# A fp32 Strassen mixture of experts on one core: the order of ScalarE's, VectorE's and the loads' work in its first pass

## The chip, the cores and the metric

The kernel runs on one core of a Trainium2 chip. The metric is the device time of one execution in microseconds (us). Engines: TensorE (PE, its weight loads PEld), VectorE (DVE), ScalarE (ACT), GpSimd (POOL), and SyncE (SP), which issues most DMAs.

## What is computed

A banded attention (4 batches, 8 heads, 768 positions, head width 64) gives `x` of 3072 rows by 512. `x` goes through a mixture of 8 experts, all of them for every row, with Sinkhorn-balanced weights `P`:

```
logits = x @ w_gate
logits = logits - logits.max()
P = np.exp(logits)
for _ in range(8):
    P /= P.sum(1, keepdims=True) + 1e-09
    P /= P.sum(0, keepdims=True) + 1e-09
    P *= N / E
for e in range(E):
    h = np.maximum(x @ w1[e], 0.0)   # w1[e]: 512 x 1024
    ye = h @ w2[e]                   # w2[e]: 1024 x 512
    out += P[:, e:e + 1] * ye
```

Everything is fp32 at the door and in the result. The case is about the experts.

## The kernel before

**Products.** The hidden units are cut into groups of 256 (31 groups, numbered 0 to 30; the first 256 units are done with the attention), the rows into three passes of 1024. A group's first layer (`x @ w1`) and its second layer (`h @ w2`) are each done as a Strassen product: seven products instead of eight, `m1` to `m7` for the first layer and `p1` to `p7` for the second, whose operands are sums and differences of quarter blocks. Each operand is held as a high part in a reduced fp32 form (`fp32r`) and a low part, the fp32 value less the high part, so one product is two output banks of three matmuls 128x128 by 512 (low by high, high by low, high by high): six matmuls.

**Stages.** The attention and the groups 0 to 3 come first. Then the first pass, the subject here: rows 0 to 1023, groups 4 to 29, taken in 13 chunks of two groups. The weights come raw from DRAM in this pass and are turned into blocks on the fly; the finished blocks are also stored to DRAM (`w_spill`), and the two later passes only load them. Group 30 closes each pass.

**The order on TensorE.** The function `plan` (L1731) yields: seven products of an even group, then p6, p4, p2 of the chunk before for its two groups (13 products: here half B), then seven of the odd group and p3, p7, p5, p1 of this chunk for its two groups (15: half A). Each engine's queue is in order: where the code uses `Ordered` (a wrapper that keeps program order on an engine) the instructions stand in the order in which the code is run.

**First layer** (`layer1_held`, L880). Products go to four PSUM banks `a` to `d`, in the order m3, m2, m1, m6, m5, m4, m7. VectorE sums them, applies relu and the expert's share, and forms operands; `high` is a cast on ScalarE, `rest` the subtraction that gives the low part, on VectorE. p6, p4 and p2 have their casts in a tail, run step by step (`tails`) while p3 to p1 of the odd group run. For even groups, p2's low part goes to POOL through the list `chores`. After each product stands `done(m)`.

**Second layer** (`held_second`, L1676). It uses two PSUM banks a product, for two groups. p3, p7, p6 and p4 are seeded: ScalarE copies the running sums into the banks (`seed`), TensorE adds to them, and ScalarE copies them back (`evict`). p5, p1 and p2 are not seeded; VectorE adds their banks to the sums. An eviction is issued when the next product of that layer, or the next first layer, comes up.

**Weight blocks** (`maker`, L1494). A generator: for each group and layer two parts, four blocks and three. POOL forms sums of the raw tile, ScalarE casts the high parts, POOL subtracts for the low parts, and SP stores the tile. `tick` (L1548) adds the time of a product, `SLOT`, to `clock[0]` and lets the maker run until its own `clock[1]` is ahead; a part is begun when `clock[0]` has come within `LEAD` (L52) of the product that uses it. Raw tiles come by `fetch` (L1448) into three tiles, on SP's queue in order; the first three are fetched when the maker starts.

Names in the trace: most instructions are recorded at L70 (the wrapper), matmuls at L126. `bank_a` to `bank_d` are the first layer's banks, `c_acc` the second layer's, `early` the running sums and the sums t3 and t4, `raw` the raw tiles, `ext` extra sums of them, `w` a tile of weight blocks, `p` and some of `x` operands of the second layer, `x` and `m` those of the first, `full` h22, h11 and d5.

Of the kernel before, what the change touches and what calls it, by code (L numbers as in the profile page):

```python
# [50 lines left out]
SLOT = 1.36  # L51
LEAD = {(0, 0): (15, 15), (0, 1): (15, 15), (1, 0): (17, 18), (1, 1): (14, 16)}  # L52
BIAS = ((None, (32, 256), (128, 352)), ((0, 384), (32, 256), (128, 352)))
# [545 lines left out]
class Moe:  # L599
# [279 lines left out]

    def layer1_held(self, x, blocks, share, full, ops, tmp, ps, tag, done, even):  # L880

# [17 lines left out]

        product("m3", "c", True, False)  # L900
        copy(out=t3, in_=c)
        done("m3")
        product("m2", "d", True, False)
        tt(out=t3, in0=t3, in1=d, op=ALU.subtract)
        done("m2")
        product("m1", "a", True, False)
        tt(out=t4, in0=a, in1=t3, op=ALU.add)
        done("m1")
        product("m6", "b", True, True)
        tt(out=b, in0=b, in1=t4, op=ALU.add)  # L910
        scaled(h22, b, 1)
        done("m6")
        product("m5", "c", False, True)
        tt(out=t3, in0=t3, in1=c, op=ALU.subtract)
        scaled(c, c, 1)
# [3 lines left out]
        rest("p3", c)  # L919
        done("m5")  # L920
        product("m4", "d", False, True)
        tt(out=t3, in0=d, in1=t3, op=ALU.add)
        scaled(d, d, 0)
# [3 lines left out]
        rest("p7", b)  # L927
        done("m4")
        product("m7", "a", False, True)
        tt(out=a, in0=a, in1=t3, op=ALU.add)  # L930
        scaled(h11, a, 0)
        rest("p1", d)
        rest("p5", d5)
        tt(out=c, in0=c, in1=d5, op=ALU.subtract)
        tt(out=a, in0=c, in1=h11, op=ALU.subtract)
        done("m7")
        yield
# [6 lines left out]
        high("p2", h11)  # L944
        if even:
            done(lambda: rest("p2", h11, Ordered(self.tc, nc.gpsimd).tensor_tensor))
        else:
            rest("p2", h11)

# [116 lines left out]
def pipeline(tc, attention, ident, moe, acc, scratch):  # L1066
# [12 lines left out]
    with ExitStack() as top:  # L1079
# [368 lines left out]
        def fetch(n, g, layer, part):  # L1448

            e, f = groups[g]  # L1450
# [40 lines left out]

        clock, hurry, ready, chores = [0.0, 0.0], [False], set(), []

        def maker():  # L1494
# [29 lines left out]
            for b in wanted:  # L1524
# [3 lines left out]
                clock[1] = max(clock[1], clock[0])  # L1528
                while chores:
                    chores.pop(0)()  # L1530
                    clock[1] += 1.3
                t = ring_tile(part)
# [28 lines left out]
        def first_layer(p, g):  # L1561
# [16 lines left out]
            if p == 0 and g < NG - 1:  # L1578
                return moe.layer1_held(ops, lambda i: block(g, 0, i), share, (full[0], full[3], full[4]), ops_of[g], tmp, mps, "h", done, g % 2 == 0)

# [83 lines left out]
        def done(m):  # L1664
            if callable(m):
                chores.append(m)
                return
            if m == "m3":
                if tails:
                    next(tails.pop(), None)  # L1670
                evict()
            if m == "m1" and seeds_next:
                seed(seeds_next.pop())
            tick()

        def held_second(gs, ks, ends=False):  # L1676
            begins = gs is chunks_of[0][0]
            seeded = () if begins or ends else SEEDED
            for n, k in enumerate(ks):
                if n and tails:  # L1680
                    next(tails[0], None)
                evict()
                if n + 1 < len(ks) and ks[n + 1] in seeded:
                    seed(ks[n + 1])
                while k == "p2" and chores:
                    chores.pop(0)()
                if k not in banks_of:
# [12 lines left out]
        def held(n, what, p, x, y):  # L1700
            if what == "first":
                follows, _, gs, ks = todo[n + 1]
                if follows == "second" and gs is not chunks_of[0][0] and ks[0] in SEEDED:
                    seeds_next.append(ks[0])
# [66 lines left out]
        hurry[0] = False  # L1771
        clock[1] = 3.0
        load_share(0, groups[PLAIN][0])
# [109 lines left out]
```

## Time and profile before

| | |
|---|---|
| time, median of 3 runs | 2187.73 us (2186.73 to 2188.72) |
| profiled execution | 2188.77 us, span 2187.0 us |
| mean granted TensorE clock | 0.99 of full speed |
| PE busy | 2081.3 us (95%), 10365 matmuls |
| DVE busy | 1420.2 us (65%) |
| ACT busy | 844.3 us (39%) |
| POOL busy | 1577.3 us (72%) |
| DMA | 477.49 MB, mean 218 GB/s |

In the trace "x6" at a row's end counts the instructions it joins; in brackets stands the idle time of the engine before the row and what ended it. Times are us from the span's start. A matmul's duration is modelled from its start on and overlaps the next.

### The profile page before, as it was taken

The page shows a single profiled execution, that of the slowest core. Times are in us where ns is not written, and L with a number is a line of the kernel's source. Part 1 is how long each engine was busy: PE and PEld are TensorE (multiplying, and loading weights), DVE is VectorE, ACT ScalarE, POOL GpSimd, SP SyncE. Part 2 cuts the span into 40 slices and gives each one's busy share as a digit, 9 for nine tenths or more (in the row PEclk, how much of TensorE's full clock was granted, in tenths as well). Part 3 has the DMA queues.
Part 4 walks back from the last instruction along what each step waited for, and adds up shares of the span by engine and source line. Part 5 has one row for each costly group of instructions (what it writes and reads, how often), then busy time and mean ns, then how long its engine had stood idle before and what let it go on. Part 6 is the DMA issues. An engine that isn't in the chain of part 4 may idle for free.

```text
span 2187.0 us, 30410 instructions
## 1 busy us (share of the span) xinstructions
PE 2081.3 (95%) x10365; PEld 1712.6 (78%) x10365; DVE 1420.2 (65%) x2526; ACT 844.3 (39%) x1772; POOL 1577.3 (72%) x1405
## 2 busy tenths in 40 slices
PE   8999997888989899899999999999999999999999
PEld 6888885667767677677888888888888888888887
DVE  8777776576676767675565555665656666655566
ACT  7778531455555555523222222222142222222221
POOL 6787973677677776785767677776767776767776
PEclk9999998999999999999999999999999999999999
DMA  6777575567666676688565555656875656555564
GB/s 151 207 224 200 161 286 187 202 226 256 250 225 228 244 247 240 245 303 319 196 214 200 190 203 197 208 185 217 294 287 184 208 200 210 202 199 198 188 208 143
DMA packets 229157, 477.49 MB, mean 218 GB/s; under 512 B 107072, under 2 KB 152576, under 8 KB 205696
## 3 DMA queue, kind: packets, MB, share of 16 engines
q1 hardware_dynamic: 228704, 474.40, 63.5%
q8 instruction: 84, 1.38, 0.3%
q0 software_dynamic: 288, 1.05, 0.1%
q14 instruction: 81, 0.66, 0.1%
HBM read 328.75 MB, written 146.64 MB: 217 GB/s over the span
## 4 chain that ended last, share of the span: by engine, by line
PE 77%; DVE 8%; POOL 5%; ACT 4%; issue 4%; DMA 2%; SPq 0%; ACTq 0%; DVEq 0%; POOLq 0%
PE c_acc L126 33%; PE bank_a L126 9%; PE bank_d L126 9%; PE bank_c L126 9%; PE bank_b L126 5%; POOL w L70 3%; PE o_t L126 2%; PE o_ps L126 1%; DVE full L70 1%; DVE p L70 1%; ACT p_sb L371 1%; PE s_ps L126 1%; DVE early L70 1%; PE y_ps L126 1%; DMA ws<-w 1%
## 5 line engine op out<-in xcount | busy, mean ns | idle before, releaser
L126 PE MATMUL c_acc<-p,w 128*128 128x512 f32 x2838 | 691.4, 395 | 35.1 <-POOL w L70 25.7
L126 PEld LDWEIGHTS c_acc<-p,w 128*128 128x128 f32 x2838 | 538.2, 190 | 160.6 <-POOL w L70 29.9
L1640 DVE TENSOR_TENSOR early<-early,c_acc 128x512 f32<-128x512 f32 x308 | 210.8, 688 | 180.4 <-PE c_acc L126 180.4
L126 PE MATMUL bank_c<-x,w 128*128 128x512 f32 x1068 | 274.5, 392 | 14.0 <-ACT w L70 8.2
L70 POOL TENSOR_TENSOR early<-raw,full 128x512 f32<-128x512 f32 x56 | 72.8, 1300 | 288.0 <-DVE raw L793 288.0
L126 PE MATMUL bank_d<-x,w 128*128 128x512 f32 x1068 | 272.9, 391 | 0.7 <-DMA x<-op_m 0.7
L126 PE MATMUL bank_a<-m,w 128*128 128x512 f32 x1068 | 271.8, 390 | 1.3 <-DMA m<-op_m 0.7
L796 ACT CAST p<-raw 128x512 fp32r<-128x512 f32 x150 | 93.1, 620 | 417.3 <-DVE raw L793 328.4
L70 POOL TENSOR_TENSOR w<-raw,w 128x512 fp32r<-128x512 f32 (+2 forms) x107 | 187.5, 1752 | 82.9 <-ACT w L70 82.9
L126 PEld LDWEIGHTS bank_c<-x,w 128*128 128x128 f32 x1068 | 201.7, 189 | 57.7 <-ACT w L70 8.6
L126 PEld LDWEIGHTS bank_d<-x,w 128*128 128x128 f32 x1068 | 201.6, 189 | 43.3 <-DMA x<-op_m 1.2
L126 PEld LDWEIGHTS bank_a<-m,w 128*128 128x128 f32 x1068 | 200.6, 188 | 44.0 <-DVE x L70 1.1
L126 PE MATMUL c_acc<-x,w 128*128 128x512 f32 x774 | 199.5, 393 | 31.5 <-ACT c_acc L70 15.9
L70 POOL TENSOR_TENSOR p<-raw,p 128x512 fp32r<-128x512 f32 x152 | 196.5, 1293 | 3.5 <-ACT p L796 3.4
L126 PEld LDWEIGHTS c_acc<-x,w 128*128 128x128 f32 x774 | 143.5, 188 | 70.1 <-ACT early L70 20.6
L70 POOL TENSOR_TENSOR p<-full,p 128x512 fp32r<-128x512 f32 x120 | 155.9, 1299 | 3.7 <-ACT p L796 3.7
L70 POOL TENSOR_TENSOR x<-full,x 128x512 fp32r<-128x512 f32 x72 | 93.0, 1292 | 66.5 <-ACT x L70 66.5
L804 DVE TENSOR_TENSOR early<-early,bank_d 128x512 f32<-128x512 f32 x63 | 43.3, 688 | 150.1 <-PE bank_d L126 150.1
L796 ACT CAST p<-full 128x512 fp32r<-128x512 f32 x121 | 75.1, 621 | 160.9 <-POOL full L70 140.4
L126 PE MATMUL bank_b<-m,w 128*128 128x512 f32 x534 | 135.5, 389 | 0.0
L126 PEld LDWEIGHTS bank_b<-m,w 128*128 128x128 f32 x534 | 100.2, 188 | 20.9
L371 ACT ACTIVATE p_sb<-p_sb,mx 128x256 f32<-128x256 f32 (+1 forms) x188 | 90.5, 484 | 22.7 <-DVE mx L366 22.1
(384 smaller groups left out, 3792.4 us busy)
## 6 DMA issues: line engine op xcount, KB each, us to landing
w<-ws SPq DMA_DIRECT2D x124, 1024.0 KB, 4.9
w<-ws SPq DMA_DIRECT2D x122, 768.0 KB, 4.3
ws<-w SPq DMA_DIRECT2D x54, 1024.0 KB, 4.6
ws<-w SPq DMA_DIRECT2D x53, 768.0 KB, 5.7
raw<-in_moe_w_dram SPq DMA_DIRECT2D x54, 512.0 KB, 4.4
x<-p_rows SPq DMA_DIRECT2D x21, 512.0 KB, 4.9
x<-op_m SPq DMA_DIRECT2D x16, 512.0 KB, 10.3
ws<-w SPq DMA_DIRECT2D x4, 1792.0 KB, 8.5
```

What stands on the lines that cost most here:

```text
L70: return lambda *args, **kw: self.tc.keep_in_program_order(op(*args, **kw))
L126: return self.tc.keep_in_program_order(self.engine.matmul(*args, **kw))
L371: scalar.activation(out=views[u], in_=views[u], func=AF.Exp, bias=mx[:, u:u + 1], scale=-1.0, accum_out=sm[:, i, j:j + 1])
L796: engine.copy(out=ops[k][:, 0], in_=src)
L804: tt(out=t3, in0=t3, in1=d, op=ALU.subtract)
L1640: nc.vector.tensor_tensor(out=sums[k][q], in0=sums[k][q], in1=bank, op=ALU.add)
```

## The change

Five edits, all for the first pass.

1. `done(m)` stands right behind its product, ahead of the copies and sums that read its bank. In `done`, an eviction stands ahead of the tail's next step; in `held_second` too.
2. Seeds: both seeded products of the coming chunk part are now seeded in the first layer, at m1 and at m6 (before: the first at m1, the others one product ahead in `held_second`).
3. p2's low part is done on VectorE for even groups too; the list `chores` goes. p5's low part stands ahead of p1's, and both ahead of the sums with m7.
4. The first three raw loads are issued by `nc.sync` itself, not by the ordered queue, so that their place on SP is the scheduler's.
5. `LEAD` is raised in seven of eight entries, and `clock[1]` starts at 2.0 instead of 3.0.

```
@@ -49,7 +49,7 @@
 SEEDED = ("p3", "p7", "p6", "p4")
 SLOT = 1.36
-LEAD = {(0, 0): (15, 15), (0, 1): (15, 15), (1, 0): (17, 18), (1, 1): (14, 16)}
+LEAD = {(0, 0): (17, 17), (0, 1): (16, 15), (1, 0): (20, 21), (1, 1): (16, 18)}
...
@@ -898,42 +898,42 @@
             engine(out=ops[k][:, 1], in0=src, in1=ops[k][:, 0], op=ALU.subtract)
 
         product("m3", "c", True, False)
+        done("m3")
         copy(out=t3, in_=c)
-        done("m3")
         product("m2", "d", True, False)
+        done("m2")
         tt(out=t3, in0=t3, in1=d, op=ALU.subtract)
-        done("m2")
         product("m1", "a", True, False)
+        done("m1")
         tt(out=t4, in0=a, in1=t3, op=ALU.add)
-        done("m1")
         product("m6", "b", True, True)
+        done("m6")
         tt(out=b, in0=b, in1=t4, op=ALU.add)
         scaled(h22, b, 1)
-        done("m6")
         product("m5", "c", False, True)
+        done("m5")
         tt(out=t3, in0=t3, in1=c, op=ALU.subtract)
         scaled(c, c, 1)
         high("p3", c)
         tt(out=b, in0=c, in1=h22, op=ALU.subtract)
         high("p7", b)
         rest("p3", c)
-        done("m5")
         product("m4", "d", False, True)
+        done("m4")
         tt(out=t3, in0=d, in1=t3, op=ALU.add)
         scaled(d, d, 0)
         tt(out=d5, in0=h22, in1=d, op=ALU.subtract)
         high("p5", d5)
         high("p1", d)
         rest("p7", b)
-        done("m4")
         product("m7", "a", False, True)
+        done("m7")
+        rest("p5", d5)
+        rest("p1", d)
         tt(out=a, in0=a, in1=t3, op=ALU.add)
         scaled(h11, a, 0)
-        rest("p1", d)
-        rest("p5", d5)
         tt(out=c, in0=c, in1=d5, op=ALU.subtract)
         tt(out=a, in0=c, in1=h11, op=ALU.subtract)
-        done("m7")
         yield
         high("p6", c)
         rest("p6", c)
@@ -942,10 +942,7 @@
         rest("p4", a)
         yield
         high("p2", h11)
-        if even:
-            done(lambda: rest("p2", h11, Ordered(self.tc, nc.gpsimd).tensor_tensor))
-        else:
-            rest("p2", h11)
+        rest("p2", h11)
 
     def layer1_strassen(self, x, w, hs, tmp, ps, tag, sums_first, beat):
 
@@ -1447,6 +1444,7 @@
 
         def fetch(n, g, layer, part):
 
+            queue = nc.sync if n < 3 else Ordered(tc, nc.sync)
             e, f = groups[g]
             raw = raw_tiles[n % 3]
...
@@ -1526,9 +1524,6 @@
                 while clock[0] < used_at[b] - LEAD[layer, part][g % 2] and not hurry[0]:
                     yield False
                 clock[1] = max(clock[1], clock[0])
-                while chores:
-                    chores.pop(0)()
-                    clock[1] += 1.3
                 t = ring_tile(part)
                 sums, parts = recipe(raw_tiles[raw_of[b] % 3], t, *b)
                 for to, x, y, op in sums:
...
@@ -1662,28 +1657,21 @@
             filled_banks.clear()
 
         def done(m):
-            if callable(m):
-                chores.append(m)
-                return
             if m == "m3":
+                evict()
                 if tails:
                     next(tails.pop(), None)
-                evict()
-            if m == "m1" and seeds_next:
-                seed(seeds_next.pop())
+            if m in ("m1", "m6") and seeds_next:
+                seed(seeds_next.pop(0))
             tick()
 
         def held_second(gs, ks, ends=False):
             begins = gs is chunks_of[0][0]
             seeded = () if begins or ends else SEEDED
             for n, k in enumerate(ks):
+                evict()
                 if n and tails:
                     next(tails[0], None)
-                evict()
-                if n + 1 < len(ks) and ks[n + 1] in seeded:
-                    seed(ks[n + 1])
-                while k == "p2" and chores:
-                    chores.pop(0)()
                 if k not in banks_of:
                     banks_of[k] = [cps.tile([P, WIDE], F32, name="c_acc", tag="c") for _ in range(2)]
                 banks = banks_of.pop(k)
@@ -1700,8 +1688,8 @@
         def held(n, what, p, x, y):
             if what == "first":
                 follows, _, gs, ks = todo[n + 1]
-                if follows == "second" and gs is not chunks_of[0][0] and ks[0] in SEEDED:
-                    seeds_next.append(ks[0])
+                if follows == "second" and gs is not chunks_of[0][0]:
+                    seeds_next.extend(k for k in ks if k in SEEDED)
                 rest = first_layer(0, x)
                 next(rest)
                 if follows != "first":
...
-        clock[1] = 3.0
+        clock[1] = 2.0
         load_share(0, groups[PLAIN][0])
```

The order of TensorE's products is the same. On three engines the instructions stand as follows.

SP, where the first pass begins. `ws3` are weight blocks of the early groups, stored to DRAM, from `w2` and `w2s`; `p_rows` a transposed table of shares, `ys` rows of result sums, `raw0` to `raw2` the first raw tiles. Before:

```order
L1299 DMA x01_170<-p_rows_207 128x1024
L1776 DMA ys6_205<-early_63 128x512
L1776 DMA ys7_206<-early_63 128x512
L1776 DMA ys5_204<-early_63 128x512
L1776 DMA ys6_205<-early_63 128x512
L1776 DMA ys7_206<-early_63 128x512
L70 DMA raw0_5681<-in_moe_w1_dram 128x4x256
L70 DMA raw1_5682<-in_moe_w1_dram 128x4x256
L70 DMA raw2_5674<-in_moe_w2_dram 128x2x512
```

After (the load of raw2 stands at the place of the third load before, behind the last `ys7` of this stretch):

```order
L1110 DMA ws3_5498<-w2_5388 128x2x256 x3
L1452 DMA raw0_5681<-in_moe_w1_dram 128x4x256
L1452 DMA raw1_5682<-in_moe_w1_dram 128x4x256
L1110 DMA ws3_5498<-w2s_5495 128x1024 x2
L1313 DMA p_rows_207<-prow_5030 128x128
L1764 DMA ys5_204<-early_63 128x512
L1313 DMA p_rows_207<-prow_5030 64x128
L1764 DMA ys6_205<-early_63 128x512
L1296 DMA x01_170<-p_rows_207 128x1024
```

The loads of raw0 and raw1 have moved ahead of the stores of `w2s`, of the shares and of the result rows.

ScalarE in half A, from p6's cast (`x00`) of the even group. `early<-c_acc` evicts, `c_acc<-early` seeds, `x10` is p4's operand, `x11` p2's, `w4` a tile of four weight blocks, `early<-bank_c` the copy of m3. Before:

```order
L70 CAST x00_169<-bank_c_8117 128x512
L70 COPY early_63<-c_acc_8149 128x512
L70 COPY early_63<-c_acc_8150 128x512
L70 CAST x10_171<-bank_a_8119 128x512
L70 COPY early_63<-c_acc_8214 128x512
L70 COPY extra0_5675<-c_acc_8215 128x512
L70 CAST w4_8247<-raw2_5674 128x4x256
L70 COPY early_63<-bank_c_8281 128x512
L70 CAST x11_172<-full3_5672 128x512
L70 COPY c_acc_8315<-early_63 128x512
L70 COPY c_acc_8316<-early_63 128x512
```

After:

```order
L70 COPY early_63<-c_acc_8153 128x512
L70 COPY early_63<-c_acc_8154 128x512
L70 CAST x00_169<-bank_c_8122 128x512
L70 COPY early_63<-c_acc_8168 128x512
L70 COPY extra0_5675<-c_acc_8169 128x512
L70 CAST x10_171<-bank_a_8124 128x512
L70 CAST w4_8237<-raw2_5674 128x4x256
L70 CAST x11_172<-full3_5672 128x512
L70 COPY early_63<-bank_c_8286 128x512
L70 COPY c_acc_8319<-early_63 128x512
L70 COPY c_acc_8320<-early_63 128x512
```

The evictions stand ahead of p6's and p4's casts, and p2's cast ahead of the copy of m3. Later in the same kind of half, from p6's cast of the odd group on (`bank_c` read, `p` written), before:

```order
L70 CAST p_8405<-bank_c_8281 128x512
L70 COPY early_63<-c_acc_8315 128x512
L70 COPY early_63<-c_acc_8316 128x512
L70 CAST p_8422<-bank_a_8283 128x512
L70 COPY early_63<-c_acc_8379 128x512
L70 COPY early_63<-c_acc_8380 128x512
L70 CAST w3_8397<-raw1_5682 128x2x2x128
L70 CAST w3_8397<-ext_5683 128x256
```

After:

```order
L70 COPY early_63<-c_acc_8319 128x512
L70 COPY early_63<-c_acc_8320 128x512
L70 CAST p_8407<-bank_c_8286 128x512
L70 CAST w3_8397<-raw1_5682 128x2x2x128
L70 CAST w3_8397<-ext_5683 128x256
L70 COPY early_63<-c_acc_8332 128x512
L70 COPY early_63<-c_acc_8333 128x512
L70 CAST p_8429<-bank_a_8288 128x512
```

The banks of p3 are evicted ahead of p6's cast, those of p7 behind it and behind the two casts of the tile `w3`.

VectorE at the beginning of half A, with `extra` the sums of p2 and `bank_d` the bank of the odd group's m2. Before:

```order
L70 TENSOR_TENSOR x00_169<-bank_c_8117,x00_169 128x512
L70 TENSOR_TENSOR x10_171<-bank_a_8119,x10_171 128x512
L70 TENSOR_TENSOR extra1_5676<-extra1_5676,c_acc_8262 128x512
L70 TENSOR_TENSOR extra2_5677<-extra2_5677,c_acc_8263 128x512
L70 TENSOR_TENSOR early_63<-early_63,bank_d_8282 128x512
L70 TENSOR_TENSOR early_63<-bank_a_8283,early_63 128x512
```

After:

```order
L70 TENSOR_TENSOR x00_169<-bank_c_8122,x00_169 128x512
L70 TENSOR_TENSOR x10_171<-bank_a_8124,x10_171 128x512
L70 TENSOR_TENSOR extra1_5676<-extra1_5676,c_acc_8264 128x512
L70 TENSOR_TENSOR extra2_5677<-extra2_5677,c_acc_8265 128x512
L70 TENSOR_TENSOR x11_172<-full3_5672,x11_172 128x512
L70 TENSOR_TENSOR early_63<-early_63,bank_d_8287 128x512
L70 TENSOR_TENSOR early_63<-bank_a_8288,early_63 128x512
```

p2's low part, with both inputs in SBUF, now stands between the evictions of p2's banks and the first sum of the odd group.

## Rows read from the trace of the kernel before

**Rows 1.** Windows by stage: PE, PEld, DVE, ACT, POOL busy, PEclk, DMA share, GB/s.
```profile
353.60:410.50 56.90, 38.32 (x133) 29.31 (x133) 30.10 (x44) 20.67 (x37) 37.52 (x39) 0.79 0.58 209
410.50:907.00 496.50, 440.03 (x1849) 348.35 (x1849) 342.99 (x514) 264.03 (x484) 358.50 (x342) 0.99 0.66 239
907.00:961.50 54.50, 49.33 (x205) 39.09 (x204) 41.10 (x60) 21.91 (x38) 38.92 (x35) 0.97 0.73 265
961.50:2187.00 1225.50, 1216.49 (x5413) 1006.03 (x5412) 731.58 (x1072) 311.03 (x523) 880.89 (x697) 1.00 0.62 214
```

**Rows 2.** PE's waits, 410.6 to 907: us in total, times, longest.
```profile
PE c_acc L126 <- POOL w L70: 22.0, 11, 2.0
```

**Rows 3.** Timeline of PE, one period: start, us, what, [idle before].
```profile
681.26 1.52 PE L126 MATMUL bank_c<-x,w 128*128 128x512 f32 x6
...
695.11 1.65 PE L126 MATMUL c_acc<-x,w 128*128 128x512 f32 x6 [1.45 <-ACT c_acc L70]
...
699.28 1.66 PE L126 MATMUL c_acc<-x,w 128*128 128x512 f32 x6 [1.16 <-ACT early L70]
...
702.15 1.52 PE L126 MATMUL bank_c<-x,w 128*128 128x512 f32 x6
...
720.50 5.76 PE L126 MATMUL c_acc<-p,w 128*128 128x512 f32 x24 [0.42 <-ACT early L70]
726.09 1.07 PE L126 MATMUL bank_c<-x,w 128*128 128x512 f32 x4
```

**Rows 4.** Timeline of POOL in the same period.
```profile
704.89 1.29 POOL L70 TENSOR_TENSOR x<-full,x 128x512 fp32r<-128x512 f32 x1 [4.96 <-ACT x L70]
...
709.05 2.41 POOL L70 TENSOR_TENSOR w<-raw,w 128x1024 fp32r<-128x1024 f32 x1
```

**Rows 5.** Timeline of ACT in the same period.
```profile
701.02 1.10 ACT L70 CAST w<-raw 128x1024 fp32r<-128x1024 f32 x1
...
714.88 0.58 ACT L70 CAST p<-bank_d 128x512 fp32r<-128x512 f32 x1
...
719.86 1.08 ACT L70 COPY early<-c_acc 128x512 f32<-128x512 f32 x2
```

**Rows 6.** Timeline of DVE in the same period.
```profile
705.14 0.69 DVE L70 TENSOR_TENSOR early<-early,bank_d 128x512 f32<-128x512 f32 x1 [2.10 <-PE bank_d L126]
...
711.71 0.68 DVE L70 TENSOR_TENSOR p<-bank_c,p 128x512 fp32r<-128x512 f32 x1
...
714.24 0.68 DVE L70 TENSOR_TENSOR p<-bank_b,p 128x512 fp32r<-128x512 f32 x1
...
718.58 0.70 DVE L70 TENSOR_TENSOR bank_a<-bank_c,full 128x512 f32<-128x512 f32 x1
```

**Rows 7.** Timeline of POOL and DVE, at 396 and at 723.
```profile
396.63 2.35 POOL L70 TENSOR_TENSOR w<-raw,w 128x1024 fp32r<-128x1024 f32 x1 [2.79 <-ACT w L70]
396.99 2.54 DVE L70 TENSOR_TENSOR p<-full,p 128x512 fp32r<-128x512 f32 x1
...
723.77 1.07 DVE L70 TENSOR_TENSOR p<-full,p 128x512 fp32r<-128x512 f32 x1 [1.62 <-ACT p L70]
```

**Rows 8.** Timeline of SP, POOL and PE where the first pass begins.
```profile
323.69 1.47 SPq L1113 DMA_DIRECT2D ws<-w  x3
...
354.21 1.70 SPq L70 DMA_DIRECT2D raw<-in_moe_w_dram  x3
...
359.14 1.40 POOL L70 TENSOR_TENSOR ext<-raw 128x256 f32<-128x256 f32 x2 [23.49 <-DMA raw<-in_moe_w_dram]
...
361.93 0.79 PE L126 MATMUL bank_c<-x,w 128*128 128x512 f32 x1 [8.18 <-ACT w L70]
...
379.65 2.93 PE L126 MATMUL bank_c<-x,w 128*128 128x512 f32 x6 [3.53 <-DVE p L70]
```

**Rows 9.** One tile, the row of shares: its store, and its landing.
```profile
L1316 SPq DMA_DIRECT2D p_rows<-prow x2: 320/406/492, 346.6 to 347.5; - x2
...
DMA to landing us min/median/max: 1.5/1.7/1.8
```

More of the change, by code (lines that the diff above doesn't have):

```diff
@@ L51 @@
 SLOT = 1.36
-LEAD = {(0, 0): (15, 15), (0, 1): (15, 15), (1, 0): (17, 18), (1, 1): (14, 16)}
+LEAD = {(0, 0): (17, 17), (0, 1): (16, 15), (1, 0): (20, 21), (1, 1): (16, 18)}
 BIAS = ((None, (32, 256), (128, 352)), ((0, 384), (32, 256), (128, 352)))
@@ L878, in layer1_scaled, with layer1_held @@
         rest("p2", h11, other)
-    def layer1_held(self, x, blocks, share, full, ops, tmp, ps, tag, done, even):
+    def layer1_held(self, x, blocks, share, full, ops, tmp, ps, tag, done):
         nc = self.nc
@@ L900, in layer1_held @@
         product("m3", "c", True, False)
+        done("m3")
         copy(out=t3, in_=c)
-        done("m3")
         product("m2", "d", True, False)
+        done("m2")
         tt(out=t3, in0=t3, in1=d, op=ALU.subtract)
-        done("m2")
         product("m1", "a", True, False)
+        done("m1")
         tt(out=t4, in0=a, in1=t3, op=ALU.add)
-        done("m1")
         product("m6", "b", True, True)
+        done("m6")
         tt(out=b, in0=b, in1=t4, op=ALU.add)
         scaled(h22, b, 1)
-        done("m6")
         product("m5", "c", False, True)
+        done("m5")
         tt(out=t3, in0=t3, in1=c, op=ALU.subtract)
@@ L919, in layer1_held @@
         rest("p3", c)
-        done("m5")
         product("m4", "d", False, True)
+        done("m4")
         tt(out=t3, in0=d, in1=t3, op=ALU.add)
@@ L927, in layer1_held @@
         rest("p7", b)
-        done("m4")
         product("m7", "a", False, True)
+        done("m7")
+        rest("p5", d5)
+        rest("p1", d)
         tt(out=a, in0=a, in1=t3, op=ALU.add)
         scaled(h11, a, 0)
-        rest("p1", d)
-        rest("p5", d5)
         tt(out=c, in0=c, in1=d5, op=ALU.subtract)
         tt(out=a, in0=c, in1=h11, op=ALU.subtract)
-        done("m7")
         yield
@@ L944, in layer1_held @@
         high("p2", h11)
[L945 to L948, printed above, removed]
+        rest("p2", h11)
     def layer1_strassen(self, x, w, hs, tmp, ps, tag, sums_first, beat):
@@ L1448, in fetch @@
         def fetch(n, g, layer, part):
+            queue = nc.sync if n < 3 else Ordered(tc, nc.sync)
             e, f = groups[g]
@@ L1490, in recipe @@
             return sums, [(flat_t, whole(n), n * FULL)]
-        clock, hurry, ready, chores = [0.0, 0.0], [False], set(), []
+        clock, hurry, ready = [0.0, 0.0], [False], set()
         def maker():
@@ L1528, in maker @@
                 clock[1] = max(clock[1], clock[0])
-                while chores:
-                    chores.pop(0)()
-                    clock[1] += 1.3
                 t = ring_tile(part)
@@ L1578, in first_layer @@
             if p == 0 and g < NG - 1:
-                return moe.layer1_held(ops, lambda i: block(g, 0, i), share, (full[0], full[3], full[4]), ops_of[g], tmp, mps, "h", done, g % 2 == 0)
+                return moe.layer1_held(ops, lambda i: block(g, 0, i), share, (full[0], full[3], full[4]), ops_of[g], tmp, mps, "h", done)
             return moe.layer1_scaled(ops, lambda i: blocks_of[g, 0, i], share, free if begins else full, ops_of[g], tmp, mps, "h",
@@ L1664, in done @@
         def done(m):
-            if callable(m):
-                chores.append(m)
-                return
             if m == "m3":
+                evict()
                 if tails:
                     next(tails.pop(), None)
-                evict()
-            if m == "m1" and seeds_next:
-                seed(seeds_next.pop())
+            if m in ("m1", "m6") and seeds_next:
+                seed(seeds_next.pop(0))
             tick()
@@ L1679, in held_second @@
             for n, k in enumerate(ks):
+                evict()
                 if n and tails:
                     next(tails[0], None)
[L1682 to L1686, printed above, removed]
                 if k not in banks_of:
@@ L1702, in held @@
                 follows, _, gs, ks = todo[n + 1]
-                if follows == "second" and gs is not chunks_of[0][0] and ks[0] in SEEDED:
-                    seeds_next.append(ks[0])
+                if follows == "second" and gs is not chunks_of[0][0]:
+                    seeds_next.extend(k for k in ks if k in SEEDED)
                 rest = first_layer(0, x)
@@ L1771, in pipeline @@
         hurry[0] = False
-        clock[1] = 3.0
+        clock[1] = 2.0
         load_share(0, groups[PLAIN][0])
```

## The prediction

> **What bounds the kernel now.** I read the stages first, then the waits, then one period in order of time on each engine.
>
> By stage [rows 1], TensorE is busy in 1216 of the 1225 us behind 961.5: nothing is to be had there. In the first pass it is not: it idles 56 of 496.5 us (410.5 to 907.0) and 19 of the 56.9 before that, those at a granted clock of 0.79. No other engine is full there: POOL 358, DVE 343, ACT 264 of 496.5. The bound is not an engine but the order in which results arrive.
>
> The waits [rows 2] name one that is late: low parts of weight blocks on POOL, 2.0 us, 11 times. The others are seen in a period.
>
> One period [rows 3] has two halves. Half B (even group: 7 first-layer products, then p6, p4, p2 of two groups, 13 products) runs from 681.26 to 702.15, half A (odd group: 7, then p3, p7, p5, p1 of two groups, 15 products) from there to 726.09. The 24 matmuls from 720.50 to 726.09 take 5.59 us: 1.36 for a product of six, and 0.15 more because TensorE starts again behind a wait. So the halves could take 17.68 and 20.40 us; they take 20.89 and 23.94. The 11 periods from 410.54 to 907.00 take 45.13 on average instead of 38.08. In half B the waits are 1.45 us for a seed and 1.16 for an eviction; in half A 2.0 for POOL and 0.42 for an eviction.
>
> The eviction of p3's banks is late because it stands in ScalarE's queue at 719.86, behind p6's cast, whose source DVE ends at 719.28 [rows 5, 6]. POOL is late because p2's low part sits in its queue and waits 4.96 us for its cast; the block behind it starts only at 709.05 [rows 4].
>
> **The start (saves 17.5 us).** TensorE starts the pass at 361.93, after a stop of 8.18 us, so from 353.75 [rows 8]: the raw tiles were issued at 354.21, behind result stores, and POOL had them at 359.14, 4.9 us later. In the new order the first two loads stand behind the stores of w2 that ended at 325.16 [rows 8]: landed by 331, and POOL, which idled from 335.65 (23.49 us before 359.14), has its five sums (0.7 each) by 340. What is late next is the first weight cast: in the new program it waits for the last row store too, issued at 347.5 and at most 1.8 us from landing [rows 9]. So cast at 349.4, low part done by 351.4: TensorE goes on without a stop, at full clock. Part of the next stop stays: the second group waited 3.53 us for p7's low part of the first [rows 8]. DVE ends that at 12.8 us behind a group's start (714.92 against 702.15 [rows 6, 3]), so the second group starts at 366.4; its third product needs the bank that p6's low part frees (last sum at 17.1, cast and low part 1.4, in all 18.7): 372.3 instead of 369.1. Its 15 products end at 391.9, with 1.9 us for the eviction of half A below. A fall of the clock in that stop could add 1.7. I take 393 for the 410.54 of before. Bounds: 391 if nothing else waits, 402 if only the 8.18 us go.
>
> **Half B (saves 3.2 us a period).** The seeds of p6 and p4 are now issued during the group's own third and fourth product, long before their use, and p6's eviction no longer stands behind p6's cast of this group. ScalarE casts p1 at 12.73 behind the half's start (714.88 against 702.15 [rows 5]), then two weight tiles, then evicts two banks (0.5 for each of these four; two copies took 1.08): the first is done at 14.8, and TensorE wants the bank at 11 x 1.36 = 14.96. So 17.7 us. The margin is 0.1 us: this is the step that fails first. Bound from the other side 20.9, all as before.
>
> **Half A (saves 0.5 us a period).** Let T be its start, 702.15 in the rows. POOL no longer holds p2's low part: it does the first second-layer block from T+2.6 to T+5.1 (2.41 us [rows 4]; T+9.3 before), then three sums (2.1) and the second block, done at T+10.2, where TensorE wants it at T+11.1. The wait of 2.0 us goes.
>
> What is late next is DVE. Its new instruction, p2's low part, stands between the evictions of p2's banks and the first sum of the group (T+2.99, at 705.14 [rows 6]). It needs p2's cast on ScalarE. There, behind half B's last sum (17.13 of 17.7, so T-0.6), come p6's cast, two evictions, p4's cast (2.0 together), a block cast (1.1 [rows 5]) and p2's cast (0.6): T+3.1. The block cast, done at T+2.6, lets POOL start its 2.41 us. The rows show what happens then: at 396.99 a low part with both inputs in SBUF met a POOL operation begun at 396.63 (2.35 us) and took 2.54 us, ending 0.55 us behind it; at 723.77 the same kind took 1.07; 0.68 is what a part read from PSUM takes [rows 6, 7]. So the new one ends 0.6 us behind POOL's, at T+5.7, and the first sum starts there, 2.7 us late. The chain behind it waits in part for TensorE, so five operations later (0.7 each) 1.5 us are left: p3's low part ends at T+11.7 instead of T+10.24, the group's last sum at T+18.4 (17.13 + 1.5, less 0.4, because p5's low part now finds POOL idle, plus 0.15 for its cast).
>
> ScalarE then does p6's cast (0.5), two weight tiles (0.9) and only then the eviction of p7's banks, done at T+20.45. TensorE wants that bank for p1 at 13 x 1.36 = T+17.68. So it starts p1 at T+20.5, 2.8 us late (earlier waits, 0.9 for p3's low part and 0.5 for p3's eviction, are inside this); with 0.15 for the restart half A takes 23.4 us instead of 23.94. What POOL gains goes to the new instruction's wait and to two weight casts ahead of an eviction.
>
> The Trainium skill has a rule for that meeting (SBUF — State Buffer, section Who interferes with whom): a VectorE instruction with two SBUF inputs and a GpSimd instruction that reads SBUF exclude each other, and the one that starts second is blocked for the whole of the first. By it the new instruction pays the rest of POOL's operation each time, as above; read as a fixed price of 1.07 us, without the rule, the time is that of rival 1. The rows at 396 agree with the rule: the end follows POOL's, not a fixed length.
>
> Bounds for the new instruction: 0.6 us (never meets POOL) and 3.0 (behind a whole 2.41 us); I take 2.5, since the casts that release POOL and DVE stand next to each other.
>
> **The sum.** A period takes 17.7 + 23.4 = 41.1 us; 45.13 - 41.1 = 4.03, times 11 = 44.3. The start gives 17.5. The last even half, 907.0 on, gives 3.2; the last odd one, with 14 closing products, 0.7, since its banks are freed by DVE behind the same chain. Behind 961.5 nothing. Together 65.7 us. The profiled execution was 2188.77 us (span 2187.0), 1.04 above the median: 2188.77 - 65.7 = 2123.1, against the median 2187.73 - 65.7 = 2122.
>
> **The rivals.**
> (1) The meeting does not happen, or costs 1.07: the last sum falls from T+18.4 to 17.3, the eviction is done at T+19.3, half A takes 22.25, the period 39.95: 11 x 1.15 = 12.7 less, 2109. For it: POOL may still be in its sums when the casts come. Against: the new order of ScalarE.
> (2) ScalarE becomes the bound: the 0.1 us of half B do not hold, since weight casts now stand ahead of evictions and each waits for POOL or a landing. If half B loses 1.5 us (a wait of 1.16 with its restart, as at 699.28 [rows 3]) and half A 1.0 more, the period is 43.6, and 27.5 us of the sum go: 2150. For it: ScalarE takes instructions in order, and the DMA engines, 0.66 busy now [rows 1], get the same bytes in a tenth less time. Against: the seeds leave the crowded places.
> (3) The start does not move as far, because a wait that the late load hides now ends last: TensorE starts at 360 instead of 353.75, 8 us less with the clock, 2130.
> (4) Slower. The pair of weight casts behind the first two seeds of half B waits for POOL's sums of a raw tile that POOL frees 2.5 us before the half: landing 4.9, three sums 2.1, so at +4.5. The pair and two seeds take 2.1, and p3's cast is due at +8.34: a slack of 1.7 us. Past it each us of landing holds back the seeds, the operand casts and TensorE once a period. The change loses when that costs 6 us a period (65.7 / 11): from landings of 12.6 us. Against: nothing in the rows lands so late.
>
> **How the numbers follow.** Forecast 0.50 (own range 2112 to 2134), rival 1 0.19, rival 2 0.18, rival 3 0.08, rival 4 0.05. 0.2% is 4.4 us, about what a measurement of this kernel can tell from no change. Faster by more: all but rival 4 and the far end of rival 2, 0.93; within it 0.02; slower 0.05. The range for 8 in 10 reaches from below rival 1 to rival 2: 2104 to 2150.
>
> **What would show it.** Right: no stop at 353.75 and the pass done near 896; p2's low parts of even groups on DVE at 2 us or more, ending with a POOL operation; TensorE's longest wait in half A at p1, for an eviction; no wait for POOL's weights. Wrong: periods near 40 with short low parts (rival 1); waits for evictions or seeds in half B (rival 2); a first product later than 356 (rival 3). If TensorE waits over 2 us for p3's low part, I mis-sized DVE's chain.

## The result, and the profile after

The changed kernel takes 2114.38 us (median of 3 runs, 2113.67 to 2115.20) against 2187.73: a ratio of 0.9665 (95% interval 0.9643 to 0.9687), 73.35 us less. The forecast was 2122, with a range of 2104 to 2150. The profiled execution took 2113.67 us, span 2111.7.

By stage (windows of the profile after; columns as in [rows 1], which they answer; the stages are cut where the same products begin):

```profile
351.50:389.43 37.93, 32.48 (x133) 25.60 (x132) 29.55 (x44) 17.91 (x33) 29.72 (x31) 0.96 0.77 281
389.43:834.20 444.77, 428.60 (x1850) 344.49 (x1849) 359.24 (x525) 264.77 (x486) 337.46 (x331) 1.00 0.73 267
834.20:884.30 50.10, 46.84 (x205) 38.13 (x204) 43.75 (x61) 21.09 (x38) 37.65 (x34) 1.00 0.79 289
884.30:2111.00 1226.70, 1218.38 (x5413) 1007.07 (x5411) 734.65 (x1073) 311.64 (x523) 881.29 (x697) 1.00 0.62 214
```

Of the 75.3 us between the two spans, the start gave 19.0 (410.54 - 353.60 = 56.9 before, 37.9 now), the 11 periods 51.7 (45.13 us each before, 444.77 / 11 = 40.43 now), the last two halves 4.5 (54.55 before, 50.1 now). Behind the pass 2.0 were given back (1225.45 before, 1227.4 now). The last 2.1 are not the change's: the program is that much earlier already where SP stores `w2` (321.61, against 323.69 before), and the first instruction that the change moves comes behind it, the load at 323.18. The two medians differ by 73.35.

TensorE's waits in the 11 periods (us in total, times, longest), in place of [rows 2]:

```profile
PE c_acc L126 <- ACT early L70: 11.1, 19, 0.9
PE c_acc L126 <- ACT p L70: 4.7, 11, 0.7
```

POOL is no longer among them. One period on TensorE (half A from 690.32, [rows 3] before):

```profile
690.32 1.52 PE L126 MATMUL bank_c<-x,w 128*128 128x512 f32 x6
...
699.84 1.52 PE L126 MATMUL c_acc<-p,w 128*128 128x512 f32 x6
701.75 4.33 PE L126 MATMUL c_acc<-p,w 128*128 128x512 f32 x18 [0.38 <-ACT p L70]
706.25 3.03 PE L126 MATMUL c_acc<-p,w 128*128 128x512 f32 x12 [0.17 <-ACT early L70]
710.16 2.12 PE L126 MATMUL c_acc<-p,w 128*128 128x512 f32 x8 [0.89 <-ACT early L70]
```

Half B runs from 672.64 to 690.32 without a wait: 17.68 us, which is 13 x 1.36. Half A takes 22.70, until 713.02, with three waits: for p3's operand (its low part, which VectorE ends at 701.60), for p3's eviction, and the longest for p7's eviction ahead of p1.

The same half on POOL and on VectorE (timelines; [rows 4, 6] before):

```profile
692.57 2.41 POOL L70 TENSOR_TENSOR w<-raw,w 128x1024 fp32r<-128x1024 f32 x1 [1.10 <-ACT w L70]
694.95 1.89 POOL L70 TENSOR_TENSOR ext<-raw 128x256 f32<-128x256 f32 x2
```

```profile
693.38 2.15 DVE L70 TENSOR_TENSOR x<-full,x 128x512 fp32r<-128x512 f32 x1
695.46 0.67 DVE L70 TENSOR_TENSOR early<-early,bank_d 128x512 f32<-128x512 f32 x1
...
700.92 0.68 DVE L70 TENSOR_TENSOR p<-bank_c,p 128x512 fp32r<-128x512 f32 x1
...
707.48 0.70 DVE L70 TENSOR_TENSOR bank_a<-bank_c,full 128x512 f32<-128x512 f32 x1
```

p2's low part is the first row of VectorE. It begins inside POOL's operation and ends at 695.53, 0.55 us behind POOL's end at 694.98. The group's first sum follows it and so begins at 695.46, though its bank was there 2.1 us earlier.

ScalarE at the end of that half ([rows 5] before):

```profile
708.21 0.59 ACT L70 CAST p<-bank_c 128x512 fp32r<-128x512 f32 x1 [1.53 <-DVE bank_a L70]
708.70 0.62 ACT L70 CAST w<-raw 128x512 fp32r<-128x512 f32 x1
709.22 0.41 ACT L70 CAST w<-ext 128x256 fp32r<-128x256 f32 x1
709.52 1.07 ACT L70 COPY early<-c_acc 128x512 f32<-128x512 f32 x2
```

The eviction of p7's banks (last row) waits behind p6's cast, which waits for VectorE's last sum, and behind two weight casts. Its first copy is what p1 waited for at 710.16.

The start, on SP, ScalarE and TensorE ([rows 8, 9] before):

```profile
323.18 1.38 SPq L1452 DMA_DIRECT2D raw<-in_moe_w_dram  x2
```

```profile
347.36 0.62 ACT L70 CAST w<-raw 128x512 fp32r<-128x512 f32 x1 [2.23 <-DMA p_rows<-prow]
```

```profile
351.50 1.52 PE L126 MATMUL bank_c<-x,w 128*128 128x512 f32 x6
...
364.35 2.08 PE L126 MATMUL bank_c<-x,w 128*128 128x512 f32 x4 [3.17 <-DVE p L70]
```

The raw tiles are fetched 31 us earlier, the first weight cast waits for the store of the shares, and TensorE goes into the pass without a stop. The second group begins 12.85 us later, behind a stop of 3.17 us.

### The profile page after: what moved, and what is told of

Same layout as the page of the kernel before. It is cut to its first block, busy times and chain, and to the rows that moved or that the text cites. A ratio compares the mean times of both kernels' runs of the same rounds, so it can differ in the third digit from the quotient of the medians.

```text
span 2111.7 us, 30417 instructions
## 1 busy us (share of the span) xinstructions
PE 2064.1 (98%) x10365; PEld 1705.6 (81%) x10365; DVE 1441.8 (68%) x2539; ACT 843.7 (40%) x1772; POOL 1554.4 (74%) x1392
## 4 chain that ended last, share of the span: by engine, by line
PE 74%; DVE 11%; ACT 5%; POOL 5%; issue 3%; DMA 1%; SPq 0%; ACTq 0%; DVEq 0%; POOLq 0%
PE c_acc L126 31%; PE bank_c L126 9%; PE bank_a L126 9%; PE bank_d L126 9%; PE bank_b L126 5%; PE o_t L126 2%; DVE early L70 2%; ACT p L70 2%; DVE full L70 2%; DVE x L70 1%; DVE p L70 1%; DVE bank_b L70 1%; DVE bank_c L70 1%; ACT w L70 1%; PE o_ps L126 1%
## 5 line engine op out<-in xcount | busy, mean ns | idle before, releaser
L126 PE MATMUL c_acc<-p,w 128*128 128x512 f32 x2838 | 682.4, 391 | 20.4 <-ACT early L70 12.0
L126 PEld LDWEIGHTS c_acc<-p,w 128*128 128x128 f32 x2838 | 529.8, 188 | 145.1 <-ACT early L70 22.4
L371 ACT ACTIVATE p_sb<-p_sb,mx 128x256 f32<-128x256 f32 (+1 forms) x188 | 90.9, 488 | 22.6 <-DVE mx L366 22.1
L802 ACT COPY early<-bank_c 128x512 f32<-128x512 f32 x63 | 37.2, 590 | 150.9 <-PE bank_c L126 150.7
```

Of the source, the lines that this page charges most:

```text
L126: return self.tc.keep_in_program_order(self.engine.matmul(*args, **kw))
L371: scalar.activation(out=views[u], in_=views[u], func=AF.Exp, bias=mx[:, u:u + 1], scale=-1.0, accum_out=sm[:, i, j:j + 1])
L802: nc.scalar.copy(out=t3, in_=c)
```

## The experiments

Each run's ratio stands to the kernel before on the same chip, whose medians there were 2188.0, 2187.5 and 2187.3 us. "After" is the changed kernel, at 0.9665.

**Each part alone, and all without one**

e1_fetch_only: the kernel before and

```
+            queue = nc.sync if n < 3 else Ordered(tc, nc.sync)
```

> The kernel before with one edit: the first three raw loads outside the ordered queue. Theory (the start is a late load, with nothing else behind it): TensorE does not stop at 353.75, so 8.2 us and the 2.3 us of lost clock go, and the second-layer weights of the first chunk, 3.3 + 1.7 us late before, come earlier too. The period stays at 45.1 us. 2172 us, between 2168 and 2179. Rival (the start needs the earlier planning of weight blocks as well, LEAD and clock): no more than the 8.2 us go, 2179 or later.

Measured 2175.83 us, 0.9945 (0.9929 to 0.9962): 12.2 us less. The stop at the beginning is gone (first product at 350.79 right behind the one before it), the second group stops 3.18 us as in the changed kernel, but the second-layer weights of the first chunk are late as before:

```profile
380.78 0.80 PE L126 MATMUL c_acc<-p,w 128*128 128x512 f32 x1 [3.26 <-ACT w L70]
383.21 2.08 PE L126 MATMUL c_acc<-p,w 128*128 128x512 f32 x4 [1.64 <-POOL w L70]
```

So the early load is worth two thirds of the start; these 4.9 us remain until other parts are added. The wait for the cast goes with the order edits (0.23 us in e6); the one for POOL is still there in e2 (2.63 us), and gone where p2's low part is off POOL too.

e3_lead_undone: the changed kernel with

```
+LEAD = {(0, 0): (15, 15), (0, 1): (15, 15), (1, 0): (17, 18), (1, 1): (14, 16)}
+        clock[1] = 3.0
```

> The changed kernel with LEAD and the first clock[1] of before. The orders of a period are the same but for one weight tile; in the first chunk the cast of the first second-layer tile falls back behind the casts of p6, p4 and p2. Theory: the period stays at 40.4 us, the first chunk gets back the waits of 3.3 and 1.6 us for that tile: 2119 us (2116 to 2122). Rival (LEAD is what the periods live on): 2130 or more.

Measured 2114.60 us, 0.9672 (0.9653 to 0.9691): no difference. Both theories missed: the first chunk did not get its waits back (24.3 us from 365.51 to 389.85; 25.1 in the changed kernel). The planner's numbers do nothing that can be measured here: with the order edits in place TensorE does not wait for that tile with the old numbers either.

e6_order_only: the kernel before with edits 1 and 2 and the order of p5's and p1's low parts; the core of it

```
             if m == "m3":
+                evict()
                 if tails:
                     next(tails.pop(), None)
-                evict()
-            if m == "m1" and seeds_next:
-                seed(seeds_next.pop())
+            if m in ("m1", "m6") and seeds_next:
+                seed(seeds_next.pop(0))
```

> The kernel before with the order edits alone: done ahead of the copies and sums, evictions ahead of the tails, both seeds in the first layer, p5's and p1's low parts ahead of the sums with m7. p2's low part stays on POOL, loads and LEAD as before. Theory: half B takes 17.7 us (20.89 before); half A still waits for POOL's second block, which stands behind p2's low part and the four sums and is done at T+13.8, so 23.4 us (23.94 before). 12 x 3.75 = 45 us less: 2143 us (2138 to 2150). Rival (ScalarE becomes the bound when weight casts stand ahead of evictions): half B above 18.5 us, 2153 or more.

Measured 2135.93 us, 0.9763 (0.9747 to 0.9780): 52.1 us less, 7 more than expected. Those 7 lie in the first chunk, which the forecast left out: it takes 49.6 us instead of 56.9, and its second-layer weight cast is waited for 0.23 us instead of 3.26, with the raw loads where they were. Half B is 17.7 us in every period, and from 505.6 to 833.34 half A is 23.2 to 23.5; in three other halves A (24.7 to 26.3 us) the mean granted clock is 0.93 or 0.94. This part carries the change. Which of its edits (evictions, seeds, the order of the low parts) does it was not tried apart.

e5_p2_vector_only: the kernel before with

```
-        if even:
-            done(lambda: rest("p2", h11, Ordered(self.tc, nc.gpsimd).tensor_tensor))
-        else:
-            rest("p2", h11)
+        rest("p2", h11)
```

> The kernel before with one edit: p2's low part on VectorE for even groups too, no instruction of it on POOL. Theory (POOL's wait of 2.0 us in half A only covered the late eviction of p3, which stands behind p6's cast and so behind VectorE's last sum): POOL's wait goes to 0, the eviction's grows by as much, and VectorE's chain is 0.3 to 0.7 us longer: half A 24.2 us instead of 23.94, the time 2191 us (2184 to 2198), no faster than before. Rival (POOL's low parts were the bound of half A by themselves): 2.0 us and its restart less in 12 halves, 2163 us.

Measured 2194.38 us, 1.0030 (1.0018 to 1.0043): slower by 6.4 us. POOL's wait is gone, as both theories have it, and nothing is won. In its place stands, in half A from 701.01 (timeline of TensorE):

```profile
710.53 3.23 PE L126 MATMUL c_acc<-p,w 128*128 128x512 f32 x12
716.63 9.79 PE L126 MATMUL c_acc<-p,w 128*128 128x512 f32 x36 [2.87 <-ACT c_acc L70]
726.26 1.07 PE L126 MATMUL bank_c<-x,w 128*128 128x512 f32 x4
```

It is not the eviction that I expected but p7's seed, which ScalarE holds behind two operand casts and two weight casts. Before the change the seed stood ahead of the two weight casts (first two rows, kernel before; then e5):

```profile
715.36 1.11 ACT L70 COPY c_acc<-early 128x512 f32<-128x512 f32 x2
716.40 0.62 ACT L70 CAST w<-raw 128x512 fp32r<-128x512 f32 x1
```

```profile
714.95 0.62 ACT L70 CAST w<-raw 128x512 fp32r<-128x512 f32 x1
715.47 0.62 ACT L70 CAST w<-ext 128x512 fp32r<-128x512 f32 x1
715.99 1.11 ACT L70 COPY c_acc<-early 128x512 f32<-128x512 f32 x2
```

So the edit does more than it says: with nothing in the list `chores`, the planner no longer adds the 1.3 us that it counted for each entry, and runs weight casts earlier. The seed starts 15.0 us behind the half's start instead of 13.2; 1.04 us of that are the two weight casts, 0.73 is VectorE's longer chain. How much of the 6.4 us each of them costs was not tried apart. The longer stop then costs a second time, by the clock (windows: length, busy times, granted clock, DMA share, GB/s):

```profile
711.00:714.00 3.00, 2.68 (x11) 1.65 (x9) 2.97 (x6) 0.64 (x2) 0.00 (x0) 1.00 0.75 317
714.00:716.00 2.00, 0.00 (x0) 0.00 (x0) 1.97 (x4) 2.00 (x5) 0.35 (x1) 1.00 0.00 0
716.00:718.00 2.00, 1.37 (x3) 1.16 (x4) 2.00 (x3) 1.10 (x3) 2.00 (x2) 0.53 0.00 0
718.00:720.00 2.00, 2.00 (x7) 1.54 (x6) 1.26 (x3) 1.10 (x3) 0.60 (x1) 0.62 0.31 131
720.00:722.00 2.00, 2.00 (x11) 1.65 (x10) 0.40 (x2) 2.00 (x5) 0.94 (x1) 1.00 0.96 393
```

TensorE idles from 713.7 to 716.6 and comes back at 0.5 (1.2 GHz); the full clock is there again by 720. Half A takes 25.25 us here. In the one half of this run in which the clock did not fall (469.68 to 494.29, mean clock 1.00) it takes 24.61, still more than before the change.

e2_p2_back_on_pool: the changed kernel without this part.

```
+            done(lambda: rest("p2", h11, Ordered(self.tc, nc.gpsimd).tensor_tensor))
```

> The changed kernel with p2's low part of even groups back on POOL, all else as changed. Theory: VectorE's chain in half A starts 2.1 us earlier, so no wait for p3's low part or p7's eviction, but POOL's second block comes at T+13.8 where TensorE wants it at T+10.9: half A 23.7 us instead of 22.7, 12 us more in all: 2126 us (2120 to 2132). Rival (the meeting of VectorE with POOL costs more than the place in POOL's queue did): half A under 22.2 us, 2108 or less.

Measured 2127.78 us, 0.9728 (0.9712 to 0.9744): 13.4 us more than the changed kernel. That is the theory's time, in part by luck. Half A takes 23.24 us where no clock falls, 0.5 us more than in the changed kernel and not 1.0; the rest comes from four halves of 24.7 to 25.9 us with a mean granted clock of 0.93. The only wait in half A is POOL, at the place that was expected (T = 659.08, TensorE):

```profile
668.60 1.75 PE L126 MATMUL c_acc<-p,w 128*128 128x512 f32 x7
672.88 9.59 PE L126 MATMUL c_acc<-p,w 128*128 128x512 f32 x41 [2.54 <-POOL w L70]
```

and POOL, which has p2's low part, four sums and then the blocks:

```profile
661.84 1.30 POOL L70 TENSOR_TENSOR x<-full,x 128x512 fp32r<-128x512 f32 x1 [4.55 <-ACT x L70]
...
666.02 2.41 POOL L70 TENSOR_TENSOR w<-raw,w 128x1024 fp32r<-128x1024 f32 x1
...
670.46 2.37 POOL L70 TENSOR_TENSOR w<-raw,w 128x1024 fp32r<-128x1024 f32 x1
```

The second block ends at 672.83, T+13.75. So the same edit loses 6.4 us by itself and gains 13.4 behind the other edits. Here too the planner's 1.3 us shift ScalarE: p7's eviction (677.24) stands ahead of the two weight casts that it waits behind in the changed kernel.

**What was left in half A**

e10_pool_in_halves: the changed kernel with POOL's operation cut in two.

```
-                    gp(out=low, in0=src, in1=high, op=ALU.subtract)
+                    for c in (slice(0, 2), slice(2, 4)) if b[1:] == (1, 0) else (slice(None),):
+                        gp(out=low[:, c], in0=src[:, c], in1=high[:, c], op=ALU.subtract)
```

> The changed kernel with POOL's low part of the four second-layer blocks done in two instructions of half the size (1.2 us each instead of 2.4). Theory (VectorE's low part from two SBUF inputs waits for the whole POOL instruction that is running, 0.55 us behind its end): it now waits for the first half alone, takes 1.0 us instead of 2.15, the chain of half A runs 1.0 us earlier: half A 21.9 us, 2105 us (2101 to 2109). Rival (both engines share the port, and the low part takes as long as POOL has work there): it still takes 2 us or more, no change, 2112 to 2117.

Measured 2103.01 us, 0.9617 (0.9599 to 0.9635): 11.4 us less than the changed kernel, half A 21.65. VectorE's low part, and POOL's two halves as one row:

```profile
686.37 1.03 DVE L70 TENSOR_TENSOR x<-full,x 128x512 fp32r<-128x512 f32 x1
```

```profile
685.55 3.01 POOL L70 TENSOR_TENSOR w<-raw,w 128x512 fp32r<-128x512 f32 x2 [1.13 <-ACT w L70]
```

The first half ends at 686.85, the low part at 687.40: 0.55 us behind it again. POOL's second half takes 1.76 us instead of 1.30. The low part does not take a length of its own; it waits out the one POOL instruction that runs when it starts, and the next one of POOL waits for it.

e8_p2_at_m6: the changed kernel with

```
-                if tails:
-                    next(tails.pop(), None)
+            if m == "m6" and tails:
+                next(tails.pop(), None)
```

> The changed kernel with p2's cast and low part made at m6 instead of m3, so that on VectorE they stand behind the first two sums and not ahead of them. Theory (the low part meets POOL's 2.4 us operation and holds the chain 2.15 us): the chain runs 1.0 us earlier, no wait for p3's low part (0.4) or p3's eviction (0.2), p1 0.8 us earlier: half A 21.9 us, 10 us less: 2104 us (2100 to 2108). Rival (the instruction costs its 0.7 us wherever it stands, and the meeting is hidden behind TensorE): no change, 2112 to 2116.

Measured 2106.54 us, 0.9627 (0.9611 to 0.9643): 7.8 us less. Half A 21.81 us, with p7's eviction its only wait (0.88). The last odd group gave 2.4 us of it back: 34.86 us instead of 32.42, the clock at 0.50 behind two stops.

e4_tail_later: the changed kernel with

```
-                if n and tails:
+                if n > (0 if ends else len(ks) - 3) and tails:
```

> The changed kernel with the casts and low parts of p6, p4, p2 one step later in half A (at p5, p1 and the next m3), so that p7's eviction stands ahead of p6's cast on ScalarE. Theory (the wait at p1, 0.9 us, is p7's eviction behind a cast that waits for VectorE's last sum): the wait goes to 0 and half A takes 21.6 us instead of 22.7, 12.7 us less in 12 halves: 2102 us (2099 to 2106). Rival (VectorE's chain bounds half A itself; freed of one wait TensorE meets the next, bank c or an operand of half B): 2112 to 2115.

Measured 2104.82 us, 0.9625 (0.9609 to 0.9641): 9.6 us less. The wait at p1 is gone; what stays is p3's operand, now 0.87, and p3's eviction, 0.16 (half A 21.8 to 22.1 us; the last odd group 34.7).

e7_both: the two edits together.

> The two edits of the two runs before together. Theory: nothing in half A is late any more, 20.5 to 20.9 us instead of 22.7, 22 to 26 us less: 2090 us (2086 to 2096). Rival (the two remove the same wait): no more than the better of them, 2100 or more.

Measured 2110.03 us, 0.9645 (0.9629 to 0.9661): worse than either. The time is the rival's, the reason is neither's. Half A came out as expected (20.75 us), but half B rose from 17.68 to between 18.7 and 19.5, by a wait for p6's eviction (TensorE):

```profile
645.66 1.66 PE L126 MATMUL c_acc<-x,w 128*128 128x512 f32 x6 [1.49 <-ACT early L70]
```

ScalarE shows why (half B from 629.05):

```profile
633.73 0.62 ACT L70 CAST w<-raw 128x512 fp32r<-128x512 f32 x1 [1.52 <-POOL raw L70]
634.26 0.61 ACT L70 CAST w<-ext 128x512 fp32r<-128x512 f32 x1
634.78 0.62 ACT L70 CAST p<-full 128x512 fp32r<-128x512 f32 x1
```

Together the edits moved the odd group's p2 cast (last row) behind weight casts that wait for POOL, and its low part into VectorE's chain of half B, so that p6's eviction starts 16.0 us behind the half's start (645.03) and not 14.0.

e9_split_places: e7 with the place of p2 chosen by group.

```
+            if m == ("m6" if odd[0] else "m3") and tails:
+                next(tails.pop(), None)
...
+                odd[0] = x % 2
```

> As e7_both, but p2's operand of the odd group is made at m3 of the next even group (as in e4_tail_later), only that of the even group at m6. Theory (in e7 the odd group's p2 cast stood behind weight casts that wait for POOL's sums of a late raw tile, its low part in VectorE's chain of half B, so that p6's eviction came 1.5 us late; the two edits as such do not stand in each other's way): half A 20.8 us, half B 17.7, 2 us less a period than the changed kernel: 2094 us (2089 to 2099). Rival (half B fails because half A got shorter, and raw tiles land too late for it): half B 18.7 us or more, 2106 or more.

Measured 2090.32 us, 0.9563 (0.9545 to 0.9582), faster than both kernels. Half B is 17.68 us again, half A 20.6 to 21.1; in the one that begins at 598.42 the eight products of the second layer stand in one row, with no wait that the profile marks (11.36 us where 8 x 1.36 is 10.88):

```profile
607.94 11.52 PE L126 MATMUL c_acc<-p,w 128*128 128x512 f32 x48
619.30 1.52 PE L126 MATMUL bank_c<-x,w 128*128 128x512 f32 x6
```

## Why the prediction held, and where its sizes were off

**The start** was forecast at 17.5 us and gave 19.0. Its steps came out as worked: no stop ahead of the pass, the shares' store as the wait that ends last, the second group 12.85 us behind the first (12.8 forecast), its third product 18.7 behind the pass's begin (18.7 forecast). The remainder is smaller: behind the third product I had 1.9 us for the eviction of the first half A, which took 1.0, with 0.6 of restarts and small waits; and the 1.1 us between 391.9 and the 393 that I took were not needed. The clock did fall (0.50 from 364.3 to 366.3, behind the stop of 3.17 us), but TensorE then still waited 1.32 us for the third product's bank, so the fall cost nothing here.

**Half B** was forecast at 17.7 and is 17.68; e6 shows that the order edits alone do it. The margin that the prediction put at 0.1 us is 0.3: the first bank of p6 is evicted 14.6 us behind the half's start at 672.64, and TensorE wants it at 14.96 (ScalarE, changed kernel):

```profile
686.67 0.59 ACT L70 COPY early<-c_acc 128x512 f32<-128x512 f32 x1
```

In e7 one cast in another place was enough to lose it (rival 2's mechanism).

**Half A** was forecast at 23.4 and is 22.7. This term is mis-sized, and is most of the difference between 65.7 and 73.35 us: 0.67 us a period, 7.4 in 11. The chain is the one that was predicted. With T = 690.32, p2's low part began at T+3.06 (T+3.1 forecast), the first sum at T+5.1 (5.7), p3's low part ended at T+11.3 (11.7), the last sum at T+17.9 (18.4), and p1 began at T+19.8 (20.5). The step that failed in size is the length of p2's low part, 2.5 us in the forecast and 2.15 measured. POOL began its operation 0.35 us earlier than forecast, because ScalarE reached the weight cast earlier, and that goes back to a row of the wrong half: the prediction let half B's last sum end 17.13 us behind the half's start, which is half A's figure. In half B it ended 16.80 us behind the start at 681.26 before the change, and 16.82 behind 672.64 after it (VectorE, before and after):

```profile
697.36 0.70 DVE L70 TENSOR_TENSOR bank_a<-bank_c,full 128x512 f32<-128x512 f32 x1
```

```profile
688.76 0.70 DVE L70 TENSOR_TENSOR bank_a<-bank_c,full 128x512 f32<-128x512 f32 x1
```

At the first sum the chain is already 0.55 us ahead of the forecast; the last 0.1 us lies on ScalarE, between the last sum and p1 (1.98 us, 2.1 forecast).

By its time alone the result lies nearer to rival 1 (2109) than to the forecast (2122). The row of 2.15 us decides between them: the meeting takes place in every period.

The prediction weighed a rule of the Trainium skill (SBUF — State Buffer, section Who interferes with whom), by which the later of the two is blocked for the whole of the first. The runs agree with it: in e10 a POOL instruction of half the length takes 1.1 us from the low part, and in e8 another place does. Rival 1 is refuted: with the low part at 1.03 us (e10), half A is 21.65 us, and it isn't that in the changed kernel. Nor was the 1.07 us that rival 1 took from the row at 723.77 a price without a meeting. That instruction began inside this one of POOL, which ended at 724.28, and ended at 724.84 (kernel before):

```profile
722.99 1.29 POOL L70 TENSOR_TENSOR w<-raw,w 128x512 fp32r<-128x512 f32 x1 [2.65 <-ACT w L70]
```

**What the sum hid.** The two halves were to save 3.2 and 0.5 us, 3.7 a period, but the sum counts 4.03: it takes the mean period of 45.13 us, and the period that was read takes 44.83. The 0.30 us, 3.3 in 11 periods, are the clock's. Four halves A of the kernel before take 24.7 to 24.8 us instead of 23.94, at a mean granted clock of 0.93. The forecast gave no reason why they should go; in the changed kernel they are gone, with 1.00 over all 11 periods.

e5 and e2 test the trade that the prediction saw in half A. It said that POOL's gain goes to the new wait. Behind the order edits that is not quite so: half A takes 23.24 us with POOL and 22.7 with VectorE, and more evenly, since the stop behind POOL, 2.5 us, in some periods brought the clock down (25.4 us in the half of e2 from 699.99). Without the order edits the trade loses: p7's seed, which before the change had filled its first bank 13.8 us behind the half's start where TensorE could have used it at 9 x 1.36 = 12.2, was late already, hidden behind POOL, and e5's order on ScalarE makes it later.

**Behind the pass** I had nothing; 2.0 us were given back. TensorE now waits 2.64 us for POOL's operands where the pass closes (1.50 before), and behind that stop the granted clock falls, which it did not before (TensorE, then windows, after):

```profile
898.91 0.50 PE L126 MATMUL o_t<-w,p 128*128 128x512 f32 x1 [2.64 <-POOL p L70]
```

```profile
901.00:903.00 2.00, 2.00 (x8) 1.69 (x7) 0.75 (x1) 0.00 (x0) 1.98 (x3) 0.50 1.00 377
```

At 903.56 TensorE is 2.07 us further behind than at the same instruction before the change, 0.5 of it by waits and 1.6 by the clock. Of the rest of the way, where 0.9 us come back and are lost again, the cause is open.

Rival 3 is out by the first product at 351.50; rival 4 was not seen: the pair of weight casts in half B waits for POOL (1.04 us at 676.84 in the changed kernel), but TensorE does not.

## What to carry to other kernels

When several waits end close to each other, price a single edit by what is late behind the wait that it removes: moving p2's low part lost 6.4 us by itself and won 13.4 behind the other edits. Look also at what else an edit moves: dropping POOL's list shifted weight casts on ScalarE. On an engine whose queue is in order, ask of each instruction what it waits for, not how long it takes: an eviction behind a cast that waits costs as much as that cast. And where an edit leaves a margin of a few tenths of a us, the next edit must be checked there first.

## What the runs showed of the hardware

A VectorE subtraction 128x512 with both inputs in SBUF that started inside a POOL instruction ended 0.55 us behind the end of that instruction, for POOL instructions of 2.41 and 1.85 us (changed kernel), 1.30 (e10) and 0.74 (e9) alike; it took 0.69 us alone. The POOL instruction that stood right behind was longer by about 0.45 us (1.76 instead of 1.30, e10).

A stop of TensorE of 2.9 us was in most periods of e5 followed by a granted clock of 0.5 for about 3 us, and in one it was not; stops of 2.5 to 2.7 us were in four of the 11 periods of e2; in the 11 periods of the changed kernel, whose longest stop is 0.9 us, the clock is 1.00.
